# Transposes of x merged into one two-bank PSUM tile with one evacuation, and the channel mixes of the full final steps placed later in the order

## The chip, the core and the metric

The kernel runs on one core of one Trainium2 chip. The metric is the time of the device in microseconds (us) from the start of the program to its end. A core has five engines with an instruction queue each: TensorE (PE in the profile; PEld is its weight load), VectorE (DVE), ScalarE (ACT), GpSimd (POOL) and SyncE (SP). [...]Matrix products land in PSUM (8 banks of 2 KB in each of the 128 partitions)[...]; ACT or DVE has to read the result out into SBUF, which is called evacuation here. DMAs are issued by SP, ACT and POOL.

## What is computed

```python
# batch 8, seq 4224, d_model 192, 8 heads of 24 channels, 7 taps
w = softmax(weight, axis=-1)                       # [8 heads, 7 taps]
x1[b, t, h, :] = sum_k w[h, k] * x[b, t - 6 + k, h, :]     # causal convolution
theta = x1 @ w_theta                               # channel mix, 192 x 192
zr, zi = x1 * cos(theta), x1 * sin(theta)
y = w_tok_r @ zr + w_tok_i @ zi                    # token mix, 4224 x 4224, per batch
u = x1 + y
out = u + relu(u @ w_ch)                           # channel mix, 192 x 192
```

Nearly all arithmetic is in the two token mixes. The kernel computes them in float16 with float32 accumulation, and the sum of products is regrouped as in Strassen's scheme (seven products in place of eight for a pair of token blocks).

## The kernel before, in words

**Tiles.** The source tokens are cut into 33 chunks of 128 (`NK`), the target tokens into 33 blocks of 128 (`NT`), which go in pairs except for one. Batch and channels are flattened to N = 1536 columns; half of them is 768 (`g` = 0 or 1: four batches each).

**A chunk** (`Chunk`) makes the right operands `z` of the token mix from 128 tokens of x. Its tasks are, in order: `conv(0)`, `conv(1)` (8 matmuls each into a PSUM tile `pc`, evacuated by ACT), `transpose(0)`, `transpose(1)` (6 PE transposes each into a tile `tp`, evacuated to half of `xT`), `theta(0)`, `theta(1)` (8 matmuls each into a tile `v`, then two sine activations on ACT that read `v`), two `product` and two `sums` on DVE. The evacuation of `transposed` is on DVE for five of the first six halves (chunk 0's second, both of chunks 1 and 2) and on ACT for all others (`by_dve`).

**A step** (`Step`) is one pair of target blocks against up to 11 chunks whose `z` are in SBUF: 7 runs of `n` chunks, 2 matmuls each (`mix`, L427), 154 matmuls in a full step. After each run but one or two, `give` (L392) adds a PSUM result `y` onto the float32 sum `pv`. There are 58 steps. The weights come by POOL's DMAs into `st`, and DVE turns and sums them into `wt` (L327, L339). In the first and later passes `pv` goes to a scratch `part` in DRAM and comes back by SP (L363).

**A final step** is the last visit to a pair. In the twelve *full* ones (`late` is false, steps 41 to 52) each block i = 0, 1 passes through: `cast` (ACT, two halves, `pv` to float16 `ub`), `cross_u` (one DMA transpose issued by ACT, L155, `ub` to `uT`), and for each half `output`: 8 matmuls `channel_mix` on PE into a tile `v` (L138), one DVE instruction that adds relu(v) onto `pv` (L464), one store to `out` by SP (L469). In the five *late* steps that follow (fewer chunks) PE does the transposes in place of the DMA (`turn_u`).

**PSUM.** `mmpool` has two buffers of two banks for all of `bp`, `pc`, `tp` and `v` (`banks`, tag `mm`); `ypool` has two for `y`. A tile takes a buffer when the previous user's reader has finished. `uT`, for chunk and output alike, has two buffers in SBUF, `pv` and the chunk's input `xw` share six ("big").

**Order.** PE, DVE, ACT and most of POOL follow the order in which the program records the instructions (`pe`, `dve`, `act`, `pool`). SP's DMAs are placed by the scheduler. Until the first 11 chunks exist, a loop written out by hand interleaves a chunk's tasks with token matmuls (`between(n)` lets n pairs of matmuls through, or up to two pairs of idle matmuls on zeros near the start). After that every step has a list of events with a place between 0 and 7 (runs), sorted by it: `pos` places a chunk's tasks, `outputs()` gives the places of a final step's work in us from the end of that step, by a planner's time of 0.324 us for a pair of matmuls (24.9 us for a full step). A negative number lies before the end.

Of the kernel before, what the change touches and what calls it, by code (L numbers as in the profile page):

```python
# [16 lines left out]
def kernel(  # L17
# [23 lines left out]
    nc = tc.nc  # L41
# [3 lines left out]
    P = nc.NUM_PARTITIONS  # L45
# [11 lines left out]
    NG = B // GB  # L57
    GC = GB * D
# [16 lines left out]
    def in_order(engine, ins):  # L75
        if engine in last:
            tc.add_manual_dep(ins.ins, last[engine].ins.name, NOSYNC, reason="order")
        last[engine] = ins
        return ins

    def pe(ins):
        return in_order("pe", ins)

    def dve(ins):
        return in_order("dve", ins)

    def act(ins):
        return in_order("act", ins)
# [20 lines left out]
    def banks(name, dtype=F32):  # L109
        return mmpool.tile([P, 2, PC if dtype == F32 else 2 * PC], dtype,  # L110
                           name=name, tag="mm")
# [6 lines left out]
    ident = constp.tile([P, P], F16, name="ident")  # L118
    R = D - P
    wth = constp.tile([P, 4, D], F16, name="wth")  # L120
    wch = constp.tile([P, 4, D], F16, name="wch")

    def channel_pieces(w):

        return ((slice(0, P), 0, w[0:P, :]), (slice(0, R), 1, w[P:D, :]),
                (slice(R, P), 2, w[0:R, :]), (slice(0, P), 3, w[R:D, :]))
# [17 lines left out]
    def evacuate(out, in_, by_dve=False):  # L144
        if by_dve:
            dve(nc.vector.tensor_copy(out=out, in_=in_))
        else:
            act(nc.scalar.activation(out=out, in_=in_, func=AT.Copy))  # L148

    def turned():  # L150
        return wk.tile([P, 12, P], F16, name="uT", tag="uT")
# [2 lines left out]

        act(nc.scalar.dma_start(out=uT, in_=u, transpose=True))  # L155

    def transposed(uT, u, by_dve=False):
        tp = banks("tp", F16)
        for k in range(6):
            pe(nc.tensor.transpose(  # L160
                tp[:, 0, k * P : (k + 1) * P], u[:, k * P : (k + 1) * P], ident
            ))
        evacuate(uT.rearrange("p k s -> p (k s)"), tp[:, 0, 0 : 6 * P], by_dve)

    Z11, T1, Z21, Z22, T2, T4, T3 = range(7)

    class Chunk:
# [50 lines left out]
                        out=xs[t0 : t0 + Q, :], in_=self.x[a * Q : (a + 1) * Q, :]  # L218
                    )

        def transpose(self, g):
            if g == 0:
                self.xT = turned()
            transposed(
                self.xT[:, 6 * g : 6 * g + 6, :], self.x[:, g * GC : (g + 1) * GC],
                0 < self.k < 3 or (self.k, g) == (0, 1),
            )

        def theta(self, g):
            v = channel_mix(self.xT[:, 6 * g : 6 * g + 6, :], wth).rearrange(  # L230
# [24 lines left out]
        def tasks(self):  # L255

            for j in range(2):
                yield lambda j=j: self.conv(j)
            for g in range(NG):
                yield lambda g=g: self.transpose(g)  # L260
            for g in range(NG):
                yield lambda g=g: self.theta(g)
            yield lambda: self.product(Z11)
            yield lambda: self.product(Z21)
            yield lambda: self.sums(0)
            yield lambda: self.sums(1)
# [3 lines left out]
    def load_chunk(k):  # L270
        if k < NK and k not in chunks:
            chunks[k] = Chunk(k, before=chunks[k - 1] if k % NW else None)
# [7 lines left out]
    class Step:  # L280
# [170 lines left out]
            ))  # L451

        def turn_u(self, i, g):
            transposed(
                self.uT[i][:, 6 * g : 6 * g + 6, :], self.ub[i][:, g * GC : (g + 1) * GC]
            )

        def cross_u(self, i):
            crossed(self.uT[i], self.ub[i])
# [14 lines left out]
        def outputs(self):  # L474

            found = []
            for i in range(len(self.tbs)):
                if not self.late:
                    at = (4 if i else 0.9 - self.time / 7) if self.pair else 0.7
                    for g in range(NG):  # L480
                        found.append((at + g, lambda i=i, g=g: self.cast(i, g)))
                        found.append((at + 10.5 + 2.8 * g,
                                      lambda i=i, g=g: self.output(i, g)))
                    found.append((at + 2, lambda i=i: self.cross_u(i)))
                    continue
                at = 1.2 if i or not self.pair else 0.6 - self.time / 7
                every, turn, mix = 2.0, 1.2, 3.6
                for g in range(NG):
                    found.append((at, lambda i=i, g=g: self.cast(i, g)))
                    found.append((at + turn, lambda i=i, g=g: self.turn_u(i, g)))  # L490
                    found.append((at + mix, lambda i=i, g=g: self.output(i, g)))
                    at += every
            return found
# [7 lines left out]
    def step_events(t):  # L501
        found = []
        s = steps[t]
        if t + 1 < NSTEP:
            found += steps[t + 1].w_tasks()
            found.append((1.6, steps[t + 1].load_rows))
            if not steps[t + 1].ahead:
                for i in steps[t + 1].adds:
                    found.append((3.3 + 1.7 * i, lambda i=i: steps[t + 1].add_x(i)))
        for s in steps[t:]:  # L510
            if s.ahead and t == s.t - (4 if s.late else 10):
                for i in s.adds:
                    found.append((3.3 + 1.7 * i, lambda s=s, i=i: s.add_x(i)))
        if t + 2 < NSTEP:
            nxt = steps[t + 2]
            for m in (1, 2):
                found.append((1.3 + 3 * (m - 1), lambda m=m: nxt.load_w(m)))
        for at, f in outputs:
            begin = at - sum(s.time for s in steps[:t])
            if 0 <= begin < steps[t].time:  # L520
                found.append((7 * begin / steps[t].time, f))
        if t >= NU - 2:
            new = [k for k in range(NK) if start[k] == t + 2 and k >= NW]
            for k in new:
                found.append((4.5, lambda k=k: load_chunk(k)))
            at = 0.1
            for k in (k for k in range(NK) if start[k] == t + 1 and k >= NW):
                pos = [0, .5, 1.3, 1.6, 2.1, 2.5, 3.1, 3.15, 3.4, 3.6]

                def add(at, j, k):  # L530
                    def go():
                        if j == 0:
                            chunks[k].todo = chunks[k].tasks()
                        next(chunks[k].todo)()
                    found.append((at, go))
                for j, p in enumerate(pos):
                    add(at + p, j, k)
                at += 2.3
        return found
# [29 lines left out]
    def idle(n):  # L569
        for _ in range(n):  # L570
            pe(nc.tensor.matmul(
                spare[:, 0, 0:BH], lhsT=noise[:, 0:P], rhs=noise, start=True, stop=True
            ))
# [47 lines left out]
    def stream():  # L621
        for t in range(NSTEP):
            yield from steps[t].mix(step_events(t))
# [5 lines left out]
    def more(n):  # L629

        for i in range(n):
            if need[0] is None:
                need[0] = next(flow, NK)
            if need[0] > ready[0]:
                return n - i
            need[0] = next(flow, NK)
        return 0
# [7 lines left out]
    for i in range(NW + 2):  # L645
        ch = chunks.get(i) if i < NW else None
        old = chunks[i - 1] if 0 < i <= NW else None

        def between(n):
            left = more(n)  # L650
            if 0 < i < 3:
                idle(min(left, 2))

        if ch:
            ch.conv(0)
        between(2)
        if old:
            old.theta(0)
        between(1)
        if ch:  # L660
            ch.conv(1)
        if i == 0:
            idle(4)
        ready[0] = i - 2
        between(2)
        if old:
            old.theta(1)
        if i == 1:
            for _, f in steps[0].w_tasks():
                f()  # L670
        if i + 3 < NW:
            load_chunk(i + 3)
        between(1)
        if ch:
            ch.transpose(0)
        if old:
            old.product(Z11)
        between(1)
        if ch:
            ch.transpose(1)  # L680
        if old:
            old.product(Z21)
        between(1)
        if old:
            old.sums(0)
        between(1)
        if old:
            old.sums(1)
        between(1)
    nc.vector.memset(wch[:, 1:3, :], 0.0)  # L690
    for rows, i, part_w in channel_pieces(moe_w_ch):
        nc.gpsimd.dma_start(out=wch[rows, i, :], in_=part_w)
    ready[0] = NK
# [2 lines left out]
    for at, f in sorted(outputs, key=lambda e: e[0]):  # L696
        if at >= sum(s.time for s in steps):
            f()
# [28 lines left out]
```

## Time and profile before

| | |
|---|---|
| median of 6 runs | 1470.27 us (1466.67 to 1489.92) |
| the profiled execution, its own time | 1477.11 us |
| span of the profile, first to last instruction | 1475.3 us |
| PE busy | 1419.3 us, 96% |
| DVE busy | 1013.0 us, 69% |
| ACT busy | 323.4 us, 22% |
| POOL busy | 436.2 us, 30% |
| token matmuls (L427) | 7656, 1290.6 us busy |

In a row of a group the numbers behind the bar are: busy time in us, mean ns of one instruction; then the idle time of that engine just before them and what ended most of it. In the waits each row says which engine and line waited for what, the total in us, how often, and the longest. The chain of waits is followed back from the last instruction, in order of time: start, length, what. The profile was taken of one execution that is 6.8 us longer than the median.

### The profile page before, as it was taken

To read this page: it belongs to the slowest core of one execution; us is meant where nothing else is said; L and a number is where in the kernel's file an instruction comes from. 1 tells how busy PE (TensorE), PEld (TensorE's weight loads), DVE (VectorE), ACT (ScalarE), POOL (GpSimd) and SP (SyncE) were. 2 spreads that over 40 slices of the span, in tenths; PEclk is the share of its full clock that TensorE was granted. 3 is DMA by queue.
4 is the path that set the end of the run, shared out by engine and by line. 5 is a ranking of instruction groups with operands and counts; after the bars stand their busy time and mean duration, and the time that the engine had idled before them with its cause. 6 is when DMAs were issued, how large, how long until landed. Compare 5 with 4: busy or idle time off the path is not lost.

```text
span 1475.3 us, 23773 instructions
## 1 busy us (share of the span) xinstructions
PE 1419.3 (96%) x9807; PEld 886.6 (60%) x9807; DVE 1013.0 (69%) x1050; ACT 323.4 (22%) x413; POOL 436.2 (30%) x655
## 2 busy tenths in 40 slices
PE   7889999999999999999999999999999999996997
PEld 4556666666666666656656566666666666664665
DVE  6884554555458687777767858768777786774675
ACT  6861111111134353000000005245001001000034
POOL 8422211111223322522413333332132123333210
PEclk9999999999999999999999999999999999998999
DMA  9976756464699999987978799999899989999993
GB/s 179 219 165 145 143 100 147 94 150 90 156 225 214 232 213 263 218 224 158 248 163 219 171 196 241 186 238 266 151 217 217 192 193 244 206 253 161 210 219 123
DMA packets 272028, 281.98 MB, mean 191 GB/s; under 512 B 106672, under 2 KB 240176, under 8 KB 271920
## 3 DMA queue, kind: packets, MB, share of 16 engines
q0 software_dynamic: 162464, 92.15, 48.1%
q1 hardware_dynamic: 71824, 178.88, 34.8%
q10 hardware_dynamic: 37632, 9.44, 4.4%
q8 instruction: 77, 1.26, 0.3%
q14 instruction: 31, 0.25, 0.1%
HBM read 245.49 MB, written 108.13 MB: 240 GB/s over the span
## 4 chain that ended last, share of the span: by engine, by line
PE 83%; DMA 6%; DVE 6%; ACT 3%; issue 2%; SPq 0%; POOL 0%; DVEq 0%; ACTq 0%
PE y L427 74%; PE v L138 5%; DMA uT<-ub 5%; DVE wt L339 2%; PE pc L200 2%; ACT z L240 2%; DVE pv L392 1%; PE tp L160 1%; DVE wt L327 1%; ACT uT L148 1%; DVE z L251 1%; DVE pv L464 1%; DMA pv<-part 0%; DVE z L245 0%; ACT pv L390 0%
## 5 line engine op out<-in xcount | busy, mean ns | idle before, releaser
L427 PE MATMUL y<-z,wt 128*128 128x384 f16 x7656 | 1290.6, 326 | 12.5 <-DVE pv L392 11.6
L427 PEld LDWEIGHTS <-wt 128*128 128x128 f16 x7656 | 740.2, 98 | 487.6 <-issue 13.8
L392 DVE TENSOR_TENSOR pv<-y,pv 128x768 f32<-128x768 f32 x324 | 308.3, 952 | 307.8 <-PE y L427 268.4
L327 DVE STREAM_TRANSPOSE wt<-st 128x1408 f16<-128x1408 f16 (+7 forms) x224 | 327.5, 1464 | 43.1 <-PE y L427 36.2
L314 POOL DMA_DIRECT2D st<-in_moe_w_tok_i_dram x232 | 132.9, 582 | 507.8 <-DVE wt L327 493.1
L314 POOL DMA_DIRECT2D st<-in_moe_w_tok_r_dram x232 | 133.0, 583 | 458.7 <-DVE wt L327 445.3
L339 DVE TENSOR_TENSOR wt<-wt 128x1408 f16<-128x1408 f16 (+7 forms) x216 | 214.8, 994 | 45.6 <-PE y L427 43.6
L148 ACT ACTIVATE z<-pc 128x768 f16<-128x768 f32 x65 | 52.9, 814 | 390.4 <-PE pc L200 390.4
L449 ACT ACTIVATE ub<-pv 128x768 f16<-128x768 f32 x66 | 52.6, 837 | 360.6 <-DVE pv L392 350.2
L138 PEld LDWEIGHTS <-uT 128*128 128x128 f16 x1056 | 91.3, 98 | 42.8 <-DMA uT<-ub 19.6
L390 ACT ACTIVATE pv<-y 128x768 f32<-128x768 f32 x66 | 53.8, 814 | 282.7 <-PE y L427 282.6
L464 DVE SCALAR_TENSOR_TENSOR pv<-v,pv 128x768 f32<-128x768 f32 x66 | 62.7, 952 | 37.2 <-PE v L138 35.2
L187 POOL DMA_DIRECT2D xw<-in_x_dram x132 | 76.6, 593 | 27.6 <-DMA xw<-xw 6.7
L374 POOL TENSOR_TENSOR pv<-pv,xr 128x1536 f32<-128x1536 f32 x24 | 74.8, 3118 | 9.1 <-issue 8.1
L148 ACT ACTIVATE uT<-tp 128x768 f16<-128x768 f16 x79 | 63.1, 816 | 63.0 <-PE tp L160 62.1
L251 DVE TENSOR_TENSOR z<-z 128x768 f16<-128x768 f16 x132 | 73.4, 556 | 3.8
L138 PE MATMUL v<-wch,uT 128*128 128x192 f16 x528 | 55.0, 248 | 18.9 <-DMA uT<-ub 17.0
L240 ACT ACTIVATE z<-v,half_pi 128x768 f16<-128x768 f32 x66 | 59.6, 904 | 42.8 <-PE v L138 42.6
L245 DVE TENSOR_TENSOR z<-z 128x1536 f16<-128x1536 f16 x66 | 60.3, 949 | 9.9 <-ACT z L240 9.9
L138 PE MATMUL v<-wth,uT 128*128 128x192 f16 x528 | 55.0, 248 | 3.0 <-ACT z L240 2.9
L240 ACT ACTIVATE z<-v 128x768 f16<-128x768 f32 x66 | 53.2, 806 | 0.0
L160 PE MATMUL tp<-ident,z 128*128 128x128 f16 x396 | 33.1, 220 | 8.5 <-ACT z L240 8.0
(43 smaller groups left out, 147.2 us busy)
## 6 DMA issues: line engine op xcount, KB each, us to landing
part<-pv SPq DMA_DIRECT2D x79, 768.0 KB, 4.4
pv<-part SPq DMA_DIRECT2D x79, 768.0 KB, 6.0
out_dram<-pv SPq DMA_DIRECT2D x66, 384.0 KB, 5.4
st<-in_moe_w_tok_r_dram POOLq DMA_DIRECT2D x136, 176.0 KB, 5.5
st<-in_moe_w_tok_i_dram POOLq DMA_DIRECT2D x136, 176.0 KB, 4.9
xs<-z SPq DMA_DIRECT2D x132, 96.0 KB, 4.4
xw<-in_x_dram POOLq DMA_DIRECT2D x121, 96.0 KB, 5.9
xr<-xs SPq DMA_DIRECT2D x24, 384.0 KB, 4.5
```

The source lines that it names most:

```text
L138: pe(nc.tensor.matmul(v[:, k, b * D : (b + 1) * D], lhsT=tT[:, 3 * k + b + i, :], rhs=w[:, 2 * b + i, :], start=(i == 0), stop=(i == 1),))
L148: act(nc.scalar.activation(out=out, in_=in_, func=AT.Copy))
L187: nc.gpsimd.dma_start(out=self.xw[lo : lo + n, h, :, :], in_=x[:, t0 : t0 + n, :].rearrange("b s d -> s b d"),)
L240: act(nc.scalar.activation(**args))
L251: dve(nc.vector.tensor_tensor(out=z[:, o, :], in0=z[:, a, :], in1=z[:, b, :], op=ALU.subtract))
L314: pool(nc.gpsimd.dma_start(out=st[a * Q : (a + 1) * Q, 0:nb, :, 0:n] .rearrange("i r bt s -> i (r bt) s"), in_=w[self.tbs[0] * P : (self.t ...
L327: dve(nc.vector.transpose(self.w[name][:, 0 : self.n, :, :], self.st[int(name[1])][:, int(name[0]) - 1, :, 0 : self.n * Q] .rearrange("p b ...
L339: dve(nc.vector.tensor_tensor(out=self.w[name][:, 0 : self.n, :, :], in0=self.w[a][:, 0 : self.n, :, :], in1=self.w[b][:, 0 : self.n, :, : ...
L374: pool(nc.gpsimd.tensor_tensor(out=self.pv[i], in0=self.pv[i], in1=xr, op=ALU.add))
L392: dve(nc.vector.tensor_tensor(out=o, in0=yv, in1=o, op=ALU.add))
L427: pe(nc.tensor.matmul(y[cn][:, q, 0:BH], lhsT=self.w[wn][:, c, :, :].rearrange("p bt i -> p (bt i)"), rhs=chunks[k].z[:, zn, q * BH : (q + ...
L464: dve(nc.vector.scalar_tensor_tensor(out=ub, in0=channel_mix(self.uT[i][:, 6 * g : 6 * g + 6, :], wch), scalar=0.0, in1=ub, op0=ALU.max, o ...
```

## The change

1. `transposed` takes a list of halves: for a chunk all 12 PE transposes go into the two banks of one `tp` tile, one bank for each half of x, and one instruction of 1536 columns evacuates both. In place of two tasks a chunk has one (`Chunk.transpose()`), behind `between(1)` and ahead of `between(2)` in the hand-written loop, and at 1.4 in `pos` (was 1.3 and 1.6); `theta` moves from 2.1 and 2.5 to 2.2 and 2.6. The evacuation is on DVE for chunks 0, 1 and 2 and on ACT for the others. The late final steps still transpose one half at a time.
2. In the full final steps the outputs of block 0 go from 7.84 and 10.64 us after the step's end to 12 and 14.7 us, those of block 1 from 14.5 and 17.3 to 17.5 and 20.2. The casts and the cross of block 1 go from 4, 5 and 6 to 1, 2 and 3. Block 0's casts and cross stay at -2.66, -1.66 and -0.66.
3. The `memset` of `wch` becomes part of DVE's fixed order, where it stood free before.

```diff
-    def transposed(uT, u, by_dve=False):
+    def transposed(uT, u, gs, by_dve=False):
         tp = banks("tp", F16)
-        for k in range(6):
-            pe(nc.tensor.transpose(
-                tp[:, 0, k * P : (k + 1) * P], u[:, k * P : (k + 1) * P], ident
-            ))
-        evacuate(uT.rearrange("p k s -> p (k s)"), tp[:, 0, 0 : 6 * P], by_dve)
+        for g in gs:
+            for k in range(6):
+                pe(nc.tensor.transpose(
+                    tp[:, g, k * P : (k + 1) * P],
+                    u[:, g * GC + k * P : g * GC + (k + 1) * P], ident,
+                ))
+        g = slice(gs[0], gs[-1] + 1)
+        evacuate(
+            uT[:, :, :].rearrange("p (g k) s -> p g (k s)", g=NG)[:, g, :],
+            tp[:, g, 0 : 6 * P], by_dve,
+        )
...
-        def transpose(self, g):
-            if g == 0:
-                self.xT = turned()
-            transposed(
-                self.xT[:, 6 * g : 6 * g + 6, :], self.x[:, g * GC : (g + 1) * GC],
-                0 < self.k < 3 or (self.k, g) == (0, 1),
-            )
+        def transpose(self):
+            self.xT = turned()
+            transposed(self.xT, self.x, range(NG), self.k < 3)
...
-                    at = (4 if i else 0.9 - self.time / 7) if self.pair else 0.7
+                    at = 1 if i or not self.pair else 0.9 - self.time / 7
                     for g in range(NG):
                         found.append((at + g, lambda i=i, g=g: self.cast(i, g)))
-                        found.append((at + 10.5 + 2.8 * g,
+                        found.append((12 + 5.5 * i + 2.7 * g,
                                       lambda i=i, g=g: self.output(i, g)))
                     found.append((at + 2, lambda i=i: self.cross_u(i)))
...
-                pos = [0, .5, 1.3, 1.6, 2.1, 2.5, 3.1, 3.15, 3.4, 3.6]
+                pos = [0, .5, 1.4, 2.2, 2.6, 3.1, 3.15, 3.4, 3.6]
...
-            ch.transpose(0)
+            ch.transpose()
         if old:
             old.product(Z11)
-        between(1)
-        if ch:
-            ch.transpose(1)
+        between(2)
         if old:
             old.product(Z21)
...
-    nc.vector.memset(wch[:, 1:3, :], 0.0)
+    dve(nc.vector.memset(wch[:, 1:3, :], 0.0))
```

More of the change, by code (lines that the diff above doesn't have):

```diff
@@ L258, in tasks @@
                 yield lambda j=j: self.conv(j)
-            for g in range(NG):
-                yield lambda g=g: self.transpose(g)
+            yield self.transpose
             for g in range(NG):
@@ L453, in turn_u @@
         def turn_u(self, i, g):
-            transposed(
-                self.uT[i][:, 6 * g : 6 * g + 6, :], self.ub[i][:, g * GC : (g + 1) * GC]
-            )
+            transposed(self.uT[i], self.ub[i], [g])
         def cross_u(self, i):
```

## The prediction, made before the changed kernel ran

> **What bounds the kernel now.** I read the engine totals first: PE is the engine to shorten, at 96% of the span. Then the PE waits by stage, because 1475.3 - 1419.3 = 56 us of PE idle time is all that reordering can win. The page and then the waits of PE in two stretches, 0 to 100 us (the first eleven chunks) and 1010 to 1410 us (the full final steps):
>
> ```profile
> PE 1419.3 (96%) x9807; PEld 886.6 (60%) x9807; DVE 1013.0 (69%) x1050; ACT 323.4 (22%) x413; POOL 436.2 (30%) x655
> L148 ACT ACTIVATE uT<-tp 128x768 f16<-128x768 f16 x79 | 63.1, 816 | 63.0 <-PE tp L160 62.1
> ```
>
> ```profile
> PE tp L160 <- ACT z L240: 8.0, 10, 1.1
> PE y L427 <- DVE pv L392: 3.6, 3, 1.8
> PE v L138 <- ACT z L240: 2.4, 7, 0.6
> ```
>
> ```profile
> PE v L138 <- DMA uT<-ub: 17.0, 6, 12.4
> PE y L427 <- DVE pv L392: 1.1, 2, 0.8
> PE v L138 <- ACT z L240: 0.5, 1, 0.5
> ```
>
> The reader is to see that the two largest waits of PE are the two that the change touches: ten waits, 8.0 us, of a transpose for ACT's sines (it needs the PSUM buffer that `theta` holds), and six waits, 17.0 us, of a channel mix for the DMA transpose. From 100 to 1010 us PE waits a few us in all, so nothing is to be had there.
>
> The busy time by stretch shows what else is full. Columns: us, then PE, PEld, DVE, ACT, POOL busy, PE clock, DMA share, GB/s.
>
> ```profile
> 60.00:80.00 20.00, 16.98 (x165) 10.86 (x162) 17.04 (x25) 16.30 (x23) 6.89 (x12) 1.00 1.01 218
> 1277.00:1306.00 29.00, 27.95 (x189) 17.73 (x187) 19.83 (x19) 3.33 (x5) 8.20 (x12) 1.00 1.09 240
> 1334.00:1378.00 44.00, 30.22 (x189) 18.68 (x188) 18.24 (x19) 3.28 (x5) 10.98 (x15) 0.84 1.15 158
> ```
>
> In the start-up ACT is nearly as full as PE (16.3 of 20 us): what PE wins there ACT may not follow. In the last final steps the DMA engines are full. The long wait, in the timeline:
>
> ```profile
> 1335.03 1.75 POOL L379 DMA_DIRECT2D part<-xs  x2
> 1335.15 1.72 ACTq L155 DMA_TRANSPOSE uT<-ub  x1
> 1338.72 15.39 ACTq L155 DMA_TRANSPOSE uT<-ub  x1
> 1356.59 1.46 PE L138 MATMUL v<-wch,uT 128*128 128x192 f16 x8 [12.38 <-DMA uT<-ub]
> ```
>
> Block 0's transpose was issued 0.12 us after an accumulating DMA of POOL and came in after 21.4 us; the median of the 24 transposes is 6.7 us, the shortest 3.2, the longest 29.3.
>
> **What the Trainium skill says.** (1) "VectorE: DVE Perf Modes", section on the TRN2 errata, prices ScalarE from PSUM at 172 + columns cycles of 1.2 GHz, VectorE at 120 + columns/mode cycles of 0.96 GHz. For 768 columns that is 783 and (mode 2) 525 ns; the trace has 816 (L148) and 558 (L146), so the prices agree within 6%. (2) "TensorE: Matmul & The Clock Gate", What's actually happening: an idle window of some 3.4 us halves PE's clock. The trace agrees: after the wait of 12.38 us the stretch shows a clock of 0.84 and 16 matmuls take 4.22 us, where other steps have 2.76. (3) "DMA: Bandwidth & Descriptors", Issuing engines are not separate DMA queues: the DMAs of SP, ACT and POOL interleave on the same 16 engines. The shares above 1 agree.
>
> **Part 1, one evacuation for a chunk.** Removed: 33 times two evacuations; added: 33 of 1536 columns. The trace has none of that size. Price by the skill: ACT (172+1536)/1.2 GHz = 1.42 us; from the row, a second instruction of a pair adds about 0.70 us where two take 1.51 to 1.57, so the sum lies between 1.42 and 1.57; I take 1.46 and gain 0.1 us a chunk on ACT. DVE is 0.56 + 0.40 = 0.96 us for 1.12. Chunk 0 gives ACT 0.8 us and takes 0.4 on DVE. In the middle of the kernel ACT and DVE hide this; it is worth nothing there. Should a `theta` there come before its evacuation, the cost would be at most 0.8 us for each of 22 chunks, but 0.8 runs, 2.9 us, stand between the tasks for 0.7 us of PE and 1.5 of ACT: I take 0.
>
> What counts is the buffer. Before, a chunk took `pc, v, pc, v, tp, tp`, and the second `tp` came one pair of matmuls after the first: its buffer was the one that `theta` of the chunk ahead had just filled, and ACT needs two sines (1.7 us) to free it. Now the whole transpose takes the buffer of `pc`, and the next claim on `theta`'s is the next chunk's `conv(0)`, up to five pairs (1.6 us) later, behind 0.66 us of transposes. So the ten waits, 8.0 us, go. What is late next is ACT: in the cycle from 70.1 to 78.0 us it is busy but for about 0.6 us, in front of the first sine. Freed PE time passes on only up to that: I take 0.55 us for each of six cycles, 3.3. The two fastest early cycles, with waits of 1.03 us each, could win 2.0, but the fourth chunk's input landed less than 1 us before its `conv` (27.13 us): 0.85. With the waits of `theta` for the complete evacuation against it (0.1 to 0.2 us in a few cycles): **start-up 4 us**. Bounds: 8.0 if ACT follows fully; a loss of 2 if `theta` waits for the last half in each cycle.
>
> **Part 2, channel mixes later.** No instruction is added. Each transpose still starts when its cast is done, since ACT does nothing else there and block 1's casts already followed the last `give` at once (1336.12, then 1337.11): issuing order on ACT is the same, and the earlier places win nothing. Block 0's mixes move 4.2 us later (26 matmuls more ahead of the first at 0.163 us), block 1's 3.3 and 2.9 us. Allowance for a transpose before PE stalls: without a stall 8.8 us became 13 for block 0 and 12.4 became about 15.5 for block 1. The chain shows how long the late ones took:
>
> ```profile
> 1277.75 10.02 DMA uT<-ub
> 1306.59 9.74 DMA uT<-ub
> 1338.72 29.25 DMA uT<-ub
> 1379.03 9.62 DMA uT<-ub
> ```
>
> The 10.02, 9.74, 9.62 and the 8.37 at 1084.03 fit into 13, so the waits of 1.05, 0.72, 0.65 and 0.84 us go: 3.3 us. The 12.38 shrinks by 4.2 at the same landing time, and the 1.39 behind it by what block 1's move leaves, 0 to 1.4. In the profiled execution: 7.5 to 8.9 us; the slow clock (about 2.2 us) goes only if the rest of the wait falls below some 3 us.
>
> What moves with the mixes: the 48 DVE instructions (L464, 952 ns each), now between other `give`s. DVE has 8 us free in each 28 us step, and `y` has a run (3.6 us) to be freed; PE waited 1.1 us for it in this stretch, I take 0 and at worst 0.5 a step, 6. On SP the 48 stores of 384 KB go 3 to 4 us later, past one load of `xr` on four or five occasions (`xr`, issued in 0.4 us, now goes ahead) and nearer to the reloads of `pv` that wait for them; these land ten and more us before use, so 0. POOL's queue is unchanged. The stores of block 1's second half now come at the end of a step and land (5.4 us) as the next block 0's transpose starts. That costs the transpose perhaps 3 us of its 13 and nothing of PE's, unless it reaches them.
>
> The median execution is 6.8 us shorter than the profiled one; I put that down to a shorter long wait. It then has some 8 us of it, clock included. Gain there 3.3 for the short waits and 2 to 4 of the long: **final steps 5.5 us**, bounds 0 and 15 (all waits and the clock) at one side, and a loss under the rival below.
>
> **Part 3**, the `memset` of 218 ns: 0; hidden in DVE's free time at 95 us, with the weights `wch` needed only at 1063 us.
>
> **Sum.** 4 + 5.5 = 9.5 us. Against the profiled execution, 1477.1 - 4 - 8 = 1465; against the median, 1470.3 - 9.5 = **1461 us**.
>
> **Rivals.** *Slower: stores against transposes.* The store that now lands during block 0's transpose does what the accumulating DMA did at 1335. For it: DMA shares of 0.98 to 1.2 and transposes from 3.2 to 29.3 us. Against it: the long one met POOL's accumulation, and block 1's transposes ran beside loads in 5 to 7 us. It decides when block 0's transpose takes over 13 us in further steps: each then costs 21.4 - 13 = 8.4 us and 2.2 of slow clock. With two such steps and the other gains of 4 + 3.3: 1470.3 - 7.3 + 21.2 = 1484 us.
>
> *ACT is the bound of the start-up.* Its 16.3 of 20 us say so. Then the tp waits become waits of `theta` for ACT and Part 1 gives 0 to 1: 1470.3 - 0.5 - 5.5 = 1464 us, no change by the bound below.
>
> *The long wait is not in the usual runs*, or comes back at full length because the stores feed it. Then Part 2 gives 0 to 3.3 us: 1470.3 - 4 - 2 = 1464 us, no change.
>
> *It does everything.* Start-up 8, final steps 14: 1448 us.
>
> **How the numbers follow.** What a measurement of this kernel can tell from no change is about 0.5%, 7.35 us: below 1462.9 is faster, above 1477.6 slower. Forecast 0.48 and "everything" 0.10 are faster: 0.58. The two rivals that leave half, 0.15 each: 0.30 the same. Stores against transposes, with a DVE order that costs PE some waits: 0.12 slower. The range goes from "everything" up to just past the cases of no gain: 1448 to 1472; what it leaves out is the slower rival and a little below.
>
> **What would show it.** Right: no tp row in PE's waits of the first 100 us, and the eleventh chunk's `conv(0)`, at 85.40 us before, at 80 to 82; an L148 row of 1536 columns at 1.42 to 1.5 us; the uT wait of PE at 3 to 9 us, in one place, and mixes 13 us after block 0's transpose is issued. Wrong: `theta` waiting for uT or z in the start-up by more than 4 us; uT waits of over 15 us, in steps that had none, with stores issued less than 5 us before; PE waits for DVE (L392, L464) of more than 5 us from 1065 to 1400.

## The result, and the profile after

| | before | after |
|---|---|---|
| median, run on the same chip in turn | 1472.06 us (38 runs) | 1459.99 us (19 runs) |
| lowest to highest | 1459.40 to 1494.09 | 1451.01 to 1466.98 |
| ratio of times, 95% interval | | 0.9925 [0.9906, 0.9945] |
| the profiled execution, its own time | 1477.11 us | 1451.01 us |

The kernel became 12.1 us faster by the medians, 11.0 by the ratio; the interval allows 8 to 14 us. The forecast was 1461, with a gain of 9.5. Executions more than 1.5% above the fastest of their kernel count as slow and are left out of all ratios and of the spreads named in the text; "lowest to highest" has them all.

The two traces must not be subtracted as they stand. The profiled execution of after is the fastest of its 19, that of before lies 5 us above its median: they differ by 26.1 us, twice the gain. What a trace shows *by itself* (a wait that is gone, the landing of one DMA) can be read; how often it happens has to come from the runs.

Engine totals and the evacuation row of the page of after:

```profile
PE 1415.2 (98%) x9809; PEld 886.6 (61%) x9809; DVE 1016.4 (70%) x1048; ACT 317.9 (22%) x382; POOL 436.8 (30%) x655
L148 ACT ACTIVATE uT<-tp 128x1536 f16<-128x1536 f16 (+1 forms) x48 | 58.3, 1217 | 66.2 <-PE tp L162 66.2
```

PE is busy for 98% of the span: 34 us are idle where there were 56. The mean of 1217 ns mixes two shapes. The groups, kept apart by shape:

```profile
L148 ACT ACTIVATE uT<-tp 128x1536 f16<-128x1536 f16 x30 | 43.8, 1460 | 51.8 <-PE tp L162 51.8
L148 ACT ACTIVATE uT<-tp 128x768 f16<-128x768 f16 x18 | 14.5, 812 | 14.4 <-PE tp L162 14.4
L146 DVE COPY uT<-tp 128x1536 f16<-128x1536 f16 x3 | 2.9, 957 | 3.2 <-PE tp L162 3.2
```

The merged evacuation takes 1460 ns on ACT and 957 on DVE. The waits of PE in the first 100 us (who waited for what; us in total, times, longest):

```profile
PE y L429 <- DVE pv L394: 3.2, 5, 1.0
PE y L429 <- ACT pv L392: 3.0, 3, 1.2
PE v L138 <- ACT z L243: 2.5, 7, 0.6
...
PE pc L207 <- DMA xw<-in_x_dram: 1.4, 1, 1.4
...
PE v L138 <- ACT uT L148: 0.8, 1, 0.8
```

The row `PE tp <- ACT z`, 8.0 us in ten waits, is gone. Part of it has come back as other rows: PE now waits 3.0 us for ACT to start `pv` (0.8 before) and 1.4 us for the input `xw` (0.3 before). The waits from 1000 to 1410 us, the answer in full:

```profile
PE v L138 <- ACT uT L148: 0.6, 2, 0.3
PE v L138 <- ACT z L243: 0.5, 1, 0.5
PE y L429 <- DVE pv L394: 0.5, 2, 0.3
```

There is no wait for a DMA transpose at all, where there were 17.0 us. The stretches that were shown for before, with the same columns (us, then PE, PEld, DVE, ACT, POOL busy, PE clock, DMA share, GB/s):

```profile
60.00:80.00 20.00, 18.39 (x178) 12.56 (x177) 19.31 (x28) 18.27 (x23) 6.84 (x12) 1.00 1.15 246
1277.00:1306.00 29.00, 29.00 (x196) 18.53 (x195) 20.18 (x20) 3.16 (x4) 8.86 (x14) 1.00 1.16 240
1334.00:1378.00 44.00, 44.00 (x308) 28.71 (x307) 30.19 (x34) 5.55 (x7) 13.77 (x21) 1.00 1.13 234
```

In the last two PE is busy all the time at full clock (the third had 30.22 of 44 us at a clock of 0.84). In the first PE wins 1.4 us of 20, and now DVE (19.31) and ACT (18.27) are full there too. The timeline around the step that held the long wait (of its rows only POOL's accumulating DMAs, ACT's DMA transposes, each with the time that the issue took, and the first mix):

```profile
1325.57 1.76 POOL L381 DMA_DIRECT2D part<-xs  x2
1325.98 1.93 ACTq L155 DMA_TRANSPOSE uT<-ub  x1
1329.62 6.54 ACTq L155 DMA_TRANSPOSE uT<-ub  x1
1335.46 1.76 POOL L381 DMA_DIRECT2D part<-xs  x2
1339.11 0.82 PE L138 MATMUL v<-wch,uT 128*128 128x192 f16 x8
```

The accumulating DMAs still stand beside the transposes. Block 0's transpose, issued at 1325.98, landed after 12.3 us, and the first mix ran 13.13 us after the issue, without a wait: 0.8 us were left. (The time from the issue of a transpose to the mix that reads it, any wait of PE taken off, is called its allowance here.) Against before this is a shorter landing *and* a larger allowance, and one trace can't say which of the two made the gain. That is what the experiments are for.

### The profile page after: what moved, and what is told of

Its sections match the earlier page's. It is cut to its first block, busy times and chain, and to the rows that moved or that the text cites. A ratio compares the mean times of both kernels' runs of the same rounds, so it can differ in the third digit from the quotient of the medians.

```text
span 1449.2 us, 23744 instructions
## 1 busy us (share of the span) xinstructions
PE 1415.2 (98%) x9809; PEld 886.6 (61%) x9809; DVE 1016.4 (70%) x1048; ACT 317.9 (22%) x382; POOL 436.8 (30%) x655
## 4 chain that ended last, share of the span: by engine, by line
PE 88%; DVE 6%; DMA 2%; ACT 2%; issue 1%; SPq 0%; POOL 0%; DVEq 0%; ACTq 0%; POOLq 0%
PE y L429 80%; PE v L138 5%; DVE wt L341 2%; PE pc L207 1%; PE tp L162 1%; DMA xw<-xw 1%; DVE pv L394 1%; DVE z L254 1%; DVE wt L329 1%; DVE z L248 1%; DMA xw<-in_x_dram 1%; ACT z L243 1%; ACT uT L148 0%; DVE pv L464 0%; SPq L224 0%
## 5 line engine op out<-in xcount | busy, mean ns | idle before, releaser
L429 PE MATMUL y<-z,wt 128*128 128x384 f16 x7656 | 1283.5, 326 | 13.5 <-DVE pv L394 10.4
L341 DVE TENSOR_TENSOR wt<-wt 128x1408 f16<-128x1408 f16 (+7 forms) x216 | 217.9, 1009 | 41.7 <-PE y L429 39.3
L464 DVE SCALAR_TENSOR_TENSOR pv<-v,pv 128x768 f32<-128x768 f32 x66 | 62.7, 952 | 20.1 <-PE v L138 18.6
L148 ACT ACTIVATE uT<-tp 128x1536 f16<-128x1536 f16 (+1 forms) x48 | 58.3, 1217 | 66.2 <-PE tp L162 66.2
L207 PE MATMUL pc<-xw,bands 96*64 96x192 f16 x528 | 35.2, 255 | 3.1 <-DMA xw<-in_x_dram 1.4
```

Source lines behind the costliest of these rows:

```text
L341: dve(nc.vector.tensor_tensor(out=self.w[name][:, 0 : self.n, :, :], in0=self.w[a][:, 0 : self.n, :, :], in1=self.w[b][:, 0 : self.n, :, : ...
L429: pe(nc.tensor.matmul(y[cn][:, q, 0:BH], lhsT=self.w[wn][:, c, :, :].rearrange("p bt i -> p (bt i)"), rhs=chunks[k].z[:, zn, q * BH : (q + ...
```

## The experiments

Each row is compared with the kernel before, run on the same chip in turn. A ratio is of times, so 0.99 is 1% less.

| run | median us | lowest to highest, runs | kernel before there | ratio [95%] |
|---|---|---|---|---|
| e1_part1_only | 1472.08 | 1462.44 to 1485.96, 22 | 1473.55 | 0.9987 [0.9961, 1.0013] |
| e2_part2_only | 1462.48 | 1455.86 to 1472.38, 15 | 1473.55 | 0.9924 [0.9900, 0.9949] |
| e3_before_acc_early | 1483.33 | 1470.72 to 1501.01, 22 | 1473.55 | 1.0050 [1.0022, 1.0079] |
| e4_before_no_acc | 1458.12 | 1456.58 to 1469.11, 10 | 1473.55 | 0.9896 [0.9865, 0.9927] |
| e5_part1_no_acc | 1456.41 | 1453.15 to 1460.50, 6 | 1474.15 | 0.9882 [0.9845, 0.9920] |
| e6_after_no_acc | 1452.42 | 1451.42 to 1453.73, 6 | 1474.15 | 0.9854 [0.9819, 0.9890] |
| e7_two_evacuations | 1456.83 | 1453.66 to 1458.69, 6 | 1474.15 | 0.9879 [0.9843, 0.9916] |
| e8_after_acc_moved | 1456.56 | 1454.67 to 1459.81, 6 | 1474.15 | 0.9882 [0.9842, 0.9922] |
| e9_after_again | 1456.53 | 1452.28 to 1463.27, 10 | 1472.31 | 0.9905 [0.9871, 0.9938] |
| e10_after_pool_adds | 1456.08 | 1455.41 to 1459.15, 7 | 1472.31 | 0.9896 [0.9856, 0.9935] |
| e11_after_3us_later | 1452.84 | 1452.35 to 1459.55, 6 | 1472.31 | 0.9885 [0.9837, 0.9932] |
| e12_later_without_part1 | 1462.48 | 1456.62 to 1465.69, 7 | 1476.44 | 0.9903 [0.9867, 0.9939] |

### Which of the two parts gives the time

**e1_part1_only**: after, with the output places of before.

```diff
-                    at = 1 if i or not self.pair else 0.9 - self.time / 7
+                    at = (4 if i else 0.9 - self.time / 7) if self.pair else 0.7
...
-                        found.append((12 + 5.5 * i + 2.7 * g,
+                        found.append((at + 10.5 + 2.8 * g,
```

> Part 1 alone (one evacuation for a chunk, the memset in order), outputs of the full final steps at their old places. Theory (the freed PSUM buffer speeds up the start-up): 4 us less than before, ratio about 0.997, the eleventh chunk's first conv near 82 us (85.40 before), uT waits of PE in the final steps as before (4 to 17 us). Rival (ACT bounds the start-up): 0 to 1 us less, ratio 0.999 to 1.000. If the two parts add up, this ratio and that of part 2 alone multiply to the 0.9925 of the whole change.

**e2_part2_only**: before, with that same edit the other way round.

> Part 2 alone (outputs and casts of the full final steps later), the transposes of a chunk in two halves as before. Theory (mixes no longer wait for the DMA transposes): 5.5 to 8 us less, ratio 0.9945 to 0.9965, PE waits for uT in 1000 to 1410 us under 9 us, start-up as before with 8 us of tp waits. Rival (the long transpose is not in usual runs): 2 to 3 us less, ratio 0.998.

Part 2 alone moves the time by 0.76%, 11.2 us, where 5.5 to 8 were expected; that is as much as the whole change. Part 1 alone moves it by 0.13%, 1.9 us, with an interval that includes no change at all. In e1's trace the final steps still wait; the PE waits from 1000 to 1410 us:

```profile
PE v L138 <- DMA uT<-ub: 11.0, 6, 5.4
```

The trace of e2 is that of its slowest run, and so it shows what later mixes do *not* cure. The start-up wait is there (the first row below, of the first 100 us), PE still waits for transposes (the second, 1000 to 1410 us; under 9 us were expected), and in the chain of waits two transposes take far more than 13 us (a third one, off the chain, takes 15.0):

```profile
PE tp L160 <- ACT z L240: 7.6, 9, 1.1
```

```profile
PE v L138 <- DMA uT<-ub: 13.5, 3, 10.2
```

```profile
1335.40 17.96 DMA uT<-ub
...
1368.93 24.46 DMA uT<-ub
```

### What makes a transpose slow

Beside every transpose over 13 us seen so far (in the traces of before, e1 and e2) accumulating DMAs of POOL were in flight. They come from `add_x`: for the five late steps x is added onto `part` ahead of time, in DRAM, by two DMAs of 384 KB of float32 for each block (9 blocks, four steps before the step that uses them, so in the steps where the DMA transposes run).

**e3_before_acc_early**: before, with those accumulations eight steps earlier.

```diff
-            if s.ahead and t == s.t - (4 if s.late else 10):
+            if s.ahead and t == s.t - (12 if s.late else 10):
```

> The kernel before, with the accumulating DMAs of x into the scratch sums of the five late steps issued 12 steps ahead (steps 41 to 45) in place of 4 (steps 49 to 53). Same work. Theory (POOL's accumulating DMAs slow the DMA transposes beside them): the transposes of the last four full steps land in 3 to 8 us (9.6 to 29.3 before), those of the steps 41 to 45 go up to about 10; no uT wait over 3 us; 2 to 8 us less than before. Rival (the general traffic near the end slows them, whatever its kind): the last transposes stay at 9 us and more, and those of steps 41 to 45 stay at 3 to 8; time as before.

The time went the other way, up by 0.5%, but the trace bears the cause out: the earlier place lies among the first full final steps, where no transpose took over 8.4 us before. There the timeline now shows, for step 43 (of its rows only those of the accumulating DMAs, the transposes and the first mix),

```profile
1104.62 1.70 POOL L379 DMA_DIRECT2D part<-xs  x2
1110.88 1.45 ACTq L155 DMA_TRANSPOSE uT<-ub  x1
1111.27 2.21 POOL L379 DMA_DIRECT2D part<-xs  x2
1114.52 15.03 ACTq L155 DMA_TRANSPOSE uT<-ub  x1
...
1131.17 1.46 PE L138 MATMUL v<-wch,uT 128*128 128x192 f16 x8 [11.22 <-DMA uT<-ub]
```

and four landings of 17.1 to 20.2 us in steps 43 and 44, while those of the last four steps, 7.6 to 29.3 us before, fell to 3.3 to 6.2. The slow transposes went where the accumulations went. The expectation missed by the size of the damage: it had the transposes of steps 41 to 45 at about 10 us and no wait over 3, and PE waited 21.3 us in all.

**e4_before_no_acc**: before, without those accumulations. It leaves x out of u in the 9 blocks of the late steps.

```diff
-            if s.ahead and t == s.t - (4 if s.late else 10):
+            if s.ahead and not s.late and t == s.t - (4 if s.late else 10):
```

> The kernel before without the 18 accumulating DMAs that add x to the nine blocks of the late steps: x is left out of u there. Theory (these DMAs slow the transposes): all 24 transposes land in 3 to 9 us, PE waits for uT under 2 us in all, 5 to 9 us less than before. Rival (traffic in general): transposes near the end still at 9 to 10 us, one of them possibly much longer; 0 to 2 us less.

1.04% less, 15.4 us by the medians (11 to 20 by the interval), with the old output places; 5 to 9 were expected. Nine of its ten runs lie within 1456.6 to 1461.4 us, where those of before spread over 22 us. From the view of the tile `uT`, the landing time of its 24 transposes:

```profile
DMA to landing us min/median/max: 3.2/6.2/8.1
```

In the two traces the executions are 1477.1 and 1457.3 us long, 19.8 us apart, and PE's waits for transposes are 17.0 us in the one and 0.5 in the other. So both most of the spread of before and some 15 us of its median come from this collision. In e4 no transpose takes over 8.1 us, though all other loads and stores are still there. The kept traces say the same as a whole: of the 336 transposes in the fourteen traces of this document 15 took over 13 us, and each of them had an accumulation in flight; of the 265 that had none, the slowest took 12.8 us. An accumulation beside a transpose is not always enough: half of the 71 that had one landed in under 9.6 us.

### What each part is worth without the collision

**e5_part1_no_acc**: e1 with e4's edit. **e6_after_no_acc**: after with e4's edit. Both leave x out of u in the same 9 blocks.

> Part 1 alone on the quiet base: as the run of before without the 18 accumulating DMAs (x is left out of u in the nine blocks of the late steps), which took 1458.1 us with a spread of a few us, but with the merged transposes. Theory (start-up 3 us shorter, as the trace of part 1 alone shows in the first cross): 1455 us, first cross near 1051.5. Rival (ACT bounds the start-up, nothing gained): 1457.5 to 1458.5.

> The changed kernel without the 18 accumulating DMAs (x left out in the nine blocks of the late steps). Theory (the later mixes are worth what collisions of transposes with accumulations cost, and little else): 1454 to 1455 us, within 1 us of part 1 alone on the same base; what separates it from the changed kernel with accumulations, 5 us, is what the collision still costs there. Rival (later mixes help by themselves, a better spread of DVE, PSUM or DMA work): 5 us and more below part 1 alone on this base.

e5 against e4 is Part 1 alone once more: 0.9882 against 0.9896, 0.14%, some 2 us, again inside the intervals; its first final transpose was issued at 1053.1 us, later than the 1051.5 expected. e6 lies 4.0 us below e5, where at most 1 was expected. e5's trace shows why: even without accumulations two transposes there take 9.5 and 9.2 us. The prediction took the old allowance of block 0 as 8.8 us throughout. It is 8.8 to 9.1 in most steps, but only 7.4 to 7.6 in three, and these two transposes stand in such steps: PE waits 3.6 us. So the later places also pay for ordinary landings. And the changed kernel stands above e6 by 4.1 to 7.6 us in the medians of its two series, 7.5 to 10.5 by the ratios: that much the accumulations still cost it.

### Is it the buffer or the evacuation that Part 1 changes

**e7_two_evacuations**: e5, with the one two-bank tile but two evacuations of 768 columns.

```diff
-        g = slice(gs[0], gs[-1] + 1)
-        evacuate(
-            uT[:, :, :].rearrange("p (g k) s -> p g (k s)", g=NG)[:, g, :],
-            tp[:, g, 0 : 6 * P], by_dve,
-        )
+        for g in gs:
+            evacuate(
+                uT[:, 6 * g : 6 * g + 6, :].rearrange("p k s -> p (k s)"),
+                tp[:, g, 0 : 6 * P], by_dve,
+            )
```

> As part 1 alone without the accumulating DMAs, with the 12 transposes in one two-bank tile, but evacuated by two instructions of 768 columns. Theory (the gain is the PSUM buffer that the second tile no longer waits for): as with one evacuation, at most 1 us more, no tp waits of PE. Rival (the gain is the fixed cost of an evacuation saved on ACT): the 3 us are lost, 1457 to 1458.

1456.83 us beside 1456.41, ratios 0.9879 and 0.9882: no difference that these intervals could show. The first 100 us have no wait of a transpose for the sines here either. What ended that wait is the claim on PSUM (one buffer instead of two in a row), not the instruction saved on ACT. The second half's six transposes also run one pair of token matmuls earlier in both; that place was not varied alone.

### Can the rest of the collision be had

**e8_after_acc_moved**: after, with the accumulations of the late steps issued in steps 38 to 40 and at the start of 41, ahead of the DMA transposes.

```diff
-            if s.ahead and t == s.t - (4 if s.late else 10):
+            early = {53: 41, 54: 38, 55: 39, 56: 40, 57: 41}
+            if s.ahead and t == (early[s.t] if s.late else s.t - 10):
+                p = 0.3 if t == 41 else 3.3
...
-                    found.append((3.3 + 1.7 * i, lambda s=s, i=i: s.add_x(i)))
+                    found.append((p + 1.7 * i, lambda s=s, i=i: s.add_x(i)))
```

> The changed kernel with the accumulating DMAs of the five late steps issued in steps 38 to 40, and those of two of them at the start of step 41, ahead of the first DMA transpose. Nothing is left out. Theory (only beside DMA transposes do the accumulations cost PE time): 1454 to 1457 us, no uT wait, spread of a few us, 3 to 6 us better than the changed kernel. Rival (accumulations cost the same wherever they are, beside chunk loads and reloads of pv): no better than the changed kernel, 1459 to 1462, with PE waits for xw or pv at 930 to 1080 us.

**e9_after_again**: after, unchanged, a second series on the chip of the next two.

> The changed kernel once more, as the yardstick for the two beside it, with another profiled execution. Theory (a rest of the collision between accumulating DMAs and DMA transposes sets the spread of 16 us between its runs): 1459 to 1461 us in the median; a profiled execution of 1458 us or more shows a uT wait of PE of 3 us or more in steps 49 to 52, one of 1452 us none.

1456.53 us, below the 1459 to 1461 expected; 0.9905, with an interval that overlaps that of the first series. Its trace, of an execution of 1452.84 us, has no wait for a transpose again, as expected of such a run, but two landings of 12.8 and 13.0 us, the first of them, block 0's, with 0.35 us left before PE would have stalled. No execution of 1458 us or more was traced.

**e10_after_pool_adds**: after, with x added in SBUF by POOL in the late steps too, in place of the accumulations.

```diff
-            self.ahead = self.late or 0 <= t + NU - NSTEP < 2
+            self.ahead = 0 <= t + NU - NSTEP < 2
```

> The changed kernel with x added to the nine blocks of the late steps by POOL in SBUF (a load of xr by SP and 3.14 us on POOL each), as in the other steps, in place of the 18 accumulating DMAs. Nothing is left out, the order on PE, DVE and ACT is the same. Theory (the accumulations were the whole of the loss): 1452.5 to 1455 us, no uT wait, spread of 3 to 5 us. Rival (in the short late steps POOL's adds and the xr loads come in the way of SP's reloads of pv): PE and DVE waits for pv after 1375 us of 4 us and more, 1456 to 1464 us.

**e11_after_3us_later**: after, with all outputs of the full final steps 3 us later still.

```diff
-                        found.append((12 + 5.5 * i + 2.7 * g,
+                        found.append((15 + 5.5 * i + 2.7 * g,
```

> The changed kernel with the outputs of the full final steps another 3 us later (15 + 5.5 i + 2.7 g): the allowance of a DMA transpose grows from about 13.4 to 16.6 us for block 0. Theory (what is lost is the part of a landing beyond its allowance): 1 to 4 us less than the changed kernel beside it, 1456 to 1459 us. Rival (the collisions are gone at 13 us, what is left is another wait): the same within 1 us. Second rival (the stores now run into the next step's transposes and reloads): 2 to 6 us more.

e8 has no wait for a transpose, but moves the cost. (Its last accumulations still overlap the first two transposes, which take 10.5 and 10.7 us.) The waits of PE from 850 to 1065 us, e8 first and after second:

```profile
PE y L429 <- DVE pv L394: 3.9, 4, 1.8
PE pc L207 <- DMA xw<-in_x_dram: 1.5, 1, 1.5
```

```profile
PE y L429 <- DVE pv L394: 1.1, 2, 0.7
```

The accumulations now stand among the last chunks, whose input comes late: 4.3 us more in these rows. e10 has no wait for a transpose either, and gives it back behind the full steps; the waits from 1375 us to the end, e10 first, after second:

```profile
PE v L138 <- DVE pv L464: 3.8, 4, 2.7
PE y L429 <- DVE pv L394: 1.8, 2, 1.5
```

```profile
...
PE v L138 <- DVE pv L464: 1.1, 3, 0.5
...
PE y L429 <- DVE pv L394: 0.4, 1, 0.4
```

That is 4.1 us more in these two rows. Both kernels come out at 1456 us, where after itself lies. e11 keeps everything in place and only raises the allowance: 1452.84 us, 3.7 us below e9 on the same chip, and about where e6 lies, which has no such accumulations. The intervals of e11 and e9 overlap, so that it beats the changed kernel is likely, not shown.

**e12_later_without_part1**: before, with e11's output places and no Part 1.

```diff
-                        found.append((at + 10.5 + 2.8 * g,
+                        found.append((15 + 5.5 * i + 2.7 * g,
```

> The outputs at 15 + 5.5 i + 2.7 g as in the run of 3 us later, but with the transposes of a chunk in two halves as in the kernel before: with the collisions out of the way, what part 1 is worth. The same places with part 1 took 1452.8 us. Theory (start-up 3.4 us shorter, as the first cross of the traces shows): 1456 us. Rival (part 1 gives the 1.7 us that lay between the two runs without accumulations): 1454.5 us. Rival (nothing): 1453 us. The first cross comes at 1053.5 to 1055 us in its trace.

Its median, 1462.48 us, missed all three times expected; it is 9.6 us above e11's, but that was another chip, on which before was slower by 4.1 us as well. Its ratio is 0.0018 above e11's, 2.6 us, well inside the intervals. Its trace and e11's differ by 3.0 us, and their first final transposes were issued at 1054.90 and 1051.97 us. In the time of the whole it bounds Part 1 no better than e1 did.

Its trace also holds the slowest landings without an accumulation in flight, 10.6 and 12.8 us, in a step where two stores of `out` were issued 0.6 and 1.7 us after block 0's transpose. They stayed within the allowance of 16 us, and PE didn't wait.

## Why the prediction was right, and where its sum was off

**The bound and the two places.** Right: PE stayed the bound, and the time came out of the two rows named (`tp` and `uT`), which are both gone. That 1461 lies within 1 us of the measured 1459.99 is in part luck: Part 1 was taken some 2 us too high, Part 2 5.7 us too low, and the median of before was 1472.06 in 38 runs, not the 1470.3 of six.

**Part 1, predicted 4 us.** Price and mechanism were right. The row of 1536 columns has 1460 ns for the 1.46 taken between the two ends; the prices of the Trainium skill's "VectorE: DVE Perf Modes", section on the TRN2 errata, gave an estimate of 1.42, which is 3% low. The ten waits went, by the buffer and not by the evacuation (e7). The eleventh `conv(0)` came at 81.86 us, 3.5 earlier, in the 80 to 82 named. What was late next was ACT as foreseen, with 3.0 us for `pv`, and the input `xw` with 1.4. In the time, the size is slightly too large: the issue of the first final transpose, a mark that all work before 1050 us precedes, lies at 1053.5 to 1054.9 us in the five traces without Part 1 and at 1049.0 to 1053.1 in the eight with it (e8, which has its accumulations ahead of that mark, left out at 1057.0). The two groups don't overlap, and their means differ by 3.5 us. In the time of the whole, the three pairs of ratios (e1, e5 with e4, e11 with e12) give 1.9, 2.1 and 2.6 us, each unresolved alone, and all below 4.

**Part 2, predicted 5.5 us, measured 11.2 (the interval of e2 gives 7.5 to 14.7).** This is the term that was mis-sized, at the step "The median execution is 6.8 us shorter than the profiled one; I put that down to a shorter long wait. It then has some 8 us of it, clock included", of which 2 to 4 were to be won. With the short waits of 3.3 us that makes 11.3 us of cost in the median execution. Taking the accumulations away lowers the *median* of before by 15.4 us (e4), and later mixes alone win 11.2: both the cost and the share of it that the change wins back were taken too low. (The upper bound of 15, "all waits and the clock", fits neither execution: it is 11.3 by the prediction's numbers for the median, and 17.0 + 2.2 = 19.2 for the profiled one.) Slow landings are no oddity of one execution: landings over 13 us were two in before's trace (21.4 and 29.25), three in e2's (15.0, 17.96 and 24.46) and three in e12's (14.0 to 17.1). But no execution near the median of before was traced, so how its cost is made up is not shown. Later mixes take up to 4.2 us off each wait of block 0, and the whole of it where the landing is within the new allowance: 13.1 us in most steps, 11.1 in three.

**The long wait does not go at its length.** "The 12.38 shrinks by 4.2 at the same landing time" is what happened where a landing stayed long: e2, with 17.96 and 24.46 us, waits 13.5 us in three places. In the trace of after no landing was longer than 12.6, so none waited: the sign named for it, a wait of 3 to 9 us in one place, did not come. That the trace was free of it is luck of that execution, the fastest of 19; the runs above it, up to 1466.98, were not caught in a trace, and that they hold such waits is inferred from e6, whose six runs spread over 2.3 us, not shown.

**The slow clock.** The forecast let it go only if the wait fell below 3 us. In after it did. What it cost in before shows in the stretch behind the long wait, where the clock is half:

```profile
1347.00:1361.00 14.00, 4.41 (x19) 2.75 (x20) 2.24 (x2) 0.00 (x0) 0.00 (x0) 0.51 1.40 132
```

PE was busy for 4.41 of 14 us, and the half clock stretched that. The Trainium skill's "TensorE: Matmul & The Clock Gate", What's actually happening, has the clock halved after an idle window of some 3.4 us. The traces agree: the eight matmuls of a mix take 1.46 us after waits of 5.38 (e1), 8.24 and 11.22 (e3), 10.19 (e2) and 12.38 us (before), but 0.83 after waits of 1.39 (before) and 1.83 (e2). No wait for a transpose between 1.94 and 5.38 us was seen, so the threshold itself is not shown here.

**The casts' earlier places, worth nothing.** Right by the order of the program, though no run varied them alone: from 1050 to 1385 us ACT runs nothing but the casts in before (48 of them) and issues the transposes, and their order among themselves is the same with the old places.

**Rivals.** *Stores against transposes* cost PE nothing in the trace of after: block 0's transposes landed in 3.2 to 12.3 us there, and PE waited 0.5 us for DVE. The slowest landing beside stores and without an accumulation in flight is the 12.8 us of e12, and PE did not wait for it. *ACT bounds the start-up* is half true: ACT and DVE are at 18.3 and 19.3 of 20 us, but the start-up still got shorter. *The long wait is not in the usual runs* is refuted by e4: the collision costs the usual run 15.4 us. *Everything* (1448) was not reached; e6, which leaves work out, and e11 are the nearest, at 1452 to 1453. The DMA share above 1, read as "the DMA engines are full", told nothing of the wait: it is 1.09 and 1.15 in the two stretches before, and 1.16 and 1.13 after, without any wait. That DMAs of different issuers meet, as the prediction has it from the skill, is shown by e3 and e4 rather than by that share: ACT's transposes slow down where POOL's accumulations are.

**What stays open.** Which property of these DMAs slows a transpose: that they accumulate, that they widen float16 to float32, that both ends lie in DRAM, their number of packets, or the traffic that they add. No run separates these. Part 1's worth in the time of the whole has no interval that excludes zero; only the mark at 1050 us separates the two groups of traces.

## What to carry to other kernels

When the profiled execution is longer than the median, don't scale its one large wait down to fit: take away what causes the wait in one run, and the drop of the median and of the spread says what it costs in all. A wait for a DMA whose landing varies is treated by allowance: ask which landings fit into the new one, and look for the transfer beside the long landings before moving it, since it may slow the neighbours of its new place. And ahead of merging two small evacuations, ask what claims the PSUM buffer next; here that claim was the gain, and the instruction saved was not.

## What the runs showed of the hardware that was not expected

- A DMA transpose of a 128x1536 float16 tile lands in 3.2 to 8.1 us beside loads and stores (e4; 12.8 at most in the other traces), and took 7.6 to 29.3 us in the last four full steps, among accumulating DMAs from DRAM to DRAM (before). The slow landings moved with these (e3).
- The accumulations beside it are slow as well: the four around the two slowest transposes of before took 18.6 to 26.6 us to land, the other fourteen 7.6 to 13.3.
- The issue itself then occupies ACT's queue: 15.39 us in before and 15.03 in e3 for the second of a pair, 1.3 to 3.9 us in e4. There ACT had nothing else to do. In e2 an issue of 6.04 us for block 0 stands in the chain of waits, between block 0's casts and block 1's, ahead of the transpose of 24.46 us.
- The run-to-run spread of this kernel, 22 us, came for the most part from this one collision: with the accumulations out, nine of ten runs of e4 lie within 4.8 us and the six of e6 within 2.3. One run of e4 (1469.11) stays unexplained.
